# A spectral gate and a GEGLU MLP in one TensorE-bound kernel: operands of the switch on GpSimd's queue, last spectral tiles inside SBUF, a ninth place for half 1's operands

## The chip, the core and the metric

The kernel runs on one core of a Trainium2 chip. The metric is the time of one execution on the device, in microseconds. Matmuls run on TensorE (PE; its weight loads are PEld), element operations on VectorE (DVE) and ScalarE (ACT). SyncE (SP) and GpSimd (POOL) issue the transfers here, each by a queue of its own; in the profile's DMA views SP's transfers are q1, GpSimd's are q0.

## The reference

```python
x = A_x                                        # 1 x 2048 x 576, fp32
g = sigmoid((x * gate_w).sum(-1, keepdims=True))
X = rfft2(x) * (w_r + 1j * w_i)                # 2048 x 289 complex
a = irfft2(X, s=(2048, 576))
h = gelu(x @ w_gate) * (x @ w_up)              # 2048 x 4608, gelu by tanh
b = h @ w_down                                 # 2048 x 576
out = g * a + (1 - g) * b
```

## The kernel before

The matmuls of the MLP and those of the spectral branch run on TensorE in turn, and everything else is laid beside them. Products are made with operands split into a high and a low part (fp32r), three matmuls for one product.

**The MLP.** The 2048 tokens are two halves of 1024; half 0 is done first. After two ordinary blocks of hidden columns come groups; each group makes its gate and up products by seven Strassen-Winograd products (L1334; L1336 for the last 64 rows of the 576) from the token operands `a11`, `a12`, `s2`, `s3`, `s1`, `a22`, `s4` (each a high part `hi`, a low part `lo` and a `tail`) and from weights. Weights are loaded into `low` and `gub` (L1279, L1288), their tails of 96 KB into `gub` or `slot` (L1313), and ScalarE and VectorE split and sum them into one of four slots (L234, L1306, L1321). gelu and the products with it follow (L1360, L1364, L918), then the down products (L933), ScalarE's scaling into one of four `stg` buffers (L965), and `put` (L946): a GpSimd DMA that adds `stg` into `yd` in DRAM.

**The switch.** The operands of half 1 are made early and kept in DRAM, in `kept`. In the last group of half 0, `swap(name)` (L1059, L1060) loads hi (512 KB), lo (512 KB) and tail (256 KB) of each name over half 0's, behind the product that read them last: 21 transfers.

**The spectral branch** is a generator. Each piece of TensorE work ends in a `gap()`, which adds to a credit what the piece took; the generators in `gens` run until the credit is used, then those in `side`. `at(n, fn)` calls `fn` n gaps later, `waits(n)` lets n gaps pass, `step(us)` takes credit. So the order of all engines is set by the credit. Its stages, in order:

- Row FFTs in `rows` (butterflies L93, L98, L101), their tiles sent to `away` in DRAM; the gates.
- `other_operands`: half 1's operands, split by ScalarE's copy (`highs`) and VectorE's subtraction (`rests`, L1138), summed (L1070) and stored to `kept` (L1144, L1151). They lie in a ring of eight places of 256 KB, handed out in turn by `place()`.
- `columns()`: the 16 column blocks kb, in four groups d=0..3 of tiles `G` in `rows`. For each kb a forward product (`product`, L336, six matmuls), a multiplication by the spectral weights `w0`, `w1` (loaded by L326), and a backward product one kb behind. `xh`, `xl` are high and low part of the forward operand (`xl` is L436), `yh`, `yl` those of the backward one (`yl` is L410). GpSimd loads the matrices `col` (L322). `beside()` does, from `side`, the four-point column steps: `forward(d)`, and `backward(d)`, which ends with the tiles of group d going to `home` in DRAM and those of group d+2 coming from `away` (`corner`, L307).
- `inverse_rows(h)`: `fetch(e)` (L634) loads row tiles from `home` into `tmp`, `wtb` and `free_low`, `spin` is their butterfly (L93, L98, L101), `settle` writes them to `rows` (L545), `inverse_stages` does the inverse row FFTs, and `adds` scales eight tiles by the gate into five places (L685 and ScalarE's L683) and adds them to `yd` by GpSimd's queue (L686). For half 0, tiles 2 and 3 of half 1 are fetched and spun at its end.
- At the end `yd` is loaded back (L987) and the last sums are made (L998).

Of the kernel before, what the change touches and what calls it, by code (L numbers as in the profile page):

```python
# [159 lines left out]
def _build(nc, tc, a):  # L160
    with ExitStack() as ctx:
# [126 lines left out]
        def columns():  # L288
# [24 lines left out]

            def store_g(d):
                for e in range(4):
                    q = SW * (d + 4 * e)
                    at(e, lambda q=q, e=e: corner(home[:, q:q + SW], G[d % 2][e], True))

# [30 lines left out]
            def backward(d):  # L349
                while done[0] < 4 * d + 3:  # L350
                    yield None
                yield None
                yield from column_four(G[d % 2], range(4), tmps, 1)
                if d:
                    yield None
                    yield from column_twiddles(G[d % 2], d, LEFT, 1, tmps)
                at(1, lambda: store_g(d))
                if d < 2:
                    yield from waits(6)
                    load_g(d + 2)  # L360
                    yield from waits(7)

# [35 lines left out]
            yield from step()  # L398
            side.append(beside())
            for kb in range(16):  # L400
                was, more = kb > 0, kb + 1 < 16
# [21 lines left out]
                u = product(1, kb - 1, yh, yl) if was else None  # L423
# [3 lines left out]
                if was:  # L427
                    copy(two(tile_of(kb - 1)), u[:, :, :NK])
                    done[0] = kb - 1
                vec.tensor_tensor(vs2[:, 0], zr, zi, ALU.add)  # L430
# [3 lines left out]
                yield from step(0.91)  # L434
                if more:
                    vec.tensor_tensor(xl, tile_of(kb + 1), f(xh), ALU.subtract)  # L436
                yield from step(0.76)
                yield from waits(STEP - 8)
            copy(yh, vs)
# [196 lines left out]
        def inverse_rows(h):  # L636
            sp = zb[0][:, 1664:1664 + SW]

            def spin(e, q):
                yield from butterfly_of(places_of(q)[0], range(4), 1, sp)  # L640

            def settle(e, q):
# [3 lines left out]
            vec.memset(rows.rearrange("p (c k) -> p c k", c=2)[:, :, 8 * KF:], 0.0)  # L646
            if h == 0:
                fetch(0)
                fetch(1)
                yield from waits(3)  # L650
                yield from spin(0, 0)
                yield from along(settle(0, 0), spin(1, 1))
                yield from settle(1, 1)
            yield from inverse_stages()
# [94 lines left out]
        def gap():  # L749
# [7 lines left out]
            if not gens:  # L757
                return
            while credit[0] > 0:
                try:  # L760
# [4 lines left out]
                if v is None:  # L765
                    while side and credit[0] > 0:
# [289 lines left out]
        def swap(name):  # L1056
            hi, lo, tail = ops[name]
            for o, q in ((hi, 0), (lo, 1)):
                nc.sync.dma_start(f(o), kept[name][:, 1024 * q:1024 * (q + 1)].rearrange("p (t k) -> p t k", t=2))  # L1059
            nc.sync.dma_start(f(tail), kept[name][:, 2048:])  # L1060

# [54 lines left out]
        def other_operands():  # L1116

            quads = ops.pop("quads")
            ring = [f(xtl[0]), zb[0][:, 1664:1664 + TB], tmp[:, 3 * TB:4 * TB], *(wtb[:, TB * i:TB * (i + 1)] for i in range(3)),
                    *(free_low[:, TB * i:TB * (i + 1)] for i in range(2))]  # L1120
# [38 lines left out]

            yield from waits(3)  # L1160
            load_xs(1, 2, quads[2])
# [476 lines left out]
```

## Time and profile before

| | |
|---|---|
| runs | 1371.89, 1372.67, 1373.62 us (median 1372.67) |
| profiled execution | 1378.64 us, span 1376.9, mean granted clock 0.987 |
| busy ACT, POOL | 841.7 (61%), 272.2 us (20%) |
| DMA | 263.31 MB in 165553 packets, 191 GB/s |
| q0 (GpSimd) | 47424 packets, 91.51 MB, 42.8% of 16 engines' span |
| q1 (SP) | 117594 packets, 170.05 MB, 38.6% |

The profile is one execution; its times count from the span's start. A granted clock under 1.00 means that TensorE ran slower for a part of a stretch. An idle time is put down to what ended it last; idle time of an engine other than TensorE matters only where TensorE then waits for it. In the chain of waits, "DMA gub<-tails" is the time from a transfer's issue to the work that it released.

### The profile page before, as it was taken

Reading aid. Unit: us, or ns where it says so; the run is one execution under the profiler, and the core shown is the slowest. Engines: PE = TensorE matmul, PEld = TensorE weight load, DVE = VectorE, ACT = ScalarE, POOL = GpSimd, SP = SyncE. Lnnn points to the kernel's source line nnn. Section 1 sums busy time; section 2 is a strip of 40 time slices with the busy share of each in tenths; the row PEclk is TensorE's granted clock in tenths of the full one; section 3 lists DMA queues with packets and bytes.
Section 4 is the critical chain, followed back from the end, with each engine's and each line's share of the span. In section 5 each row is a group of like instructions: output and inputs, shape, how many; then the busy total and the mean of one; then the engine's idle time right before and its main releaser. Section 6 shows DMA issues by size and latency. Waiting matters only on the chain.

```text
span 1376.9 us, 20502 instructions
## 1 busy us (share of the span) xinstructions
PE 1328.2 (96%) x7210; PEld 1164.7 (85%) x7210; DVE 1137.3 (83%) x1750; ACT 841.7 (61%) x1419; POOL 272.2 (20%) x339
## 2 busy tenths in 40 slices
PE   9999999999999988999799999999999999799997
PEld 7888888888888876888678888888788888688896
DVE  7889889879999967596768867876899996699974
ACT  5665655675555657676567767776555557456551
POOL 0011111211111211222221122221111114111132
PEclk9999999999999999999999999999999999899999
DMA  9669998887777899989995797887877779576799
GB/s 348 208 161 218 198 220 190 190 222 137 134 137 136 212 290 253 246 181 289 273 242 137 207 214 162 188 203 152 198 129 136 136 133 240 110 136 132 135 189 230
DMA packets 165553, 263.31 MB, mean 191 GB/s; under 512 B 14346, under 2 KB 79178, under 8 KB 164426
## 3 DMA queue, kind: packets, MB, share of 16 engines
q0 software_dynamic: 47424, 91.51, 42.8%
q1 hardware_dynamic: 117594, 170.05, 38.6%
q8 instruction: 56, 0.92, 0.3%
q10 hardware_dynamic: 432, 0.44, 0.1%
q14 instruction: 47, 0.39, 0.1%
HBM read 141.23 MB, written 123.08 MB: 192 GB/s over the span
## 4 chain that ended last, share of the span: by engine, by line
PE 73%; DMA 16%; DVE 6%; ACT 2%; issue 1%; SPq 0%; DVEq 0%; ACTq 0%
PE pdn L933 25%; PE pgu L1334 18%; PE px L1334 18%; PE pgu L1336 3%; PE px L1336 3%; DMA gub<-tails 3%; DMA tails<-wtb 3%; DMA slot<-tails 2%; DMA tmp<-home 2%; PE pdn L336 1%; DMA wtb<-wt 1%; DMA til<-kept_s 1%; DMA gub<-wf 1%; DMA xlo<-kept_a 1%; DMA tmp<-xs 1%
## 5 line engine op out<-in xcount | busy, mean ns | idle before, releaser
L946 POOL DMA_DIRECT2D yd<-stg x264 | 227.1, 862 | 1040.5 <-ACT stg L965 916.5
L965 ACT ACTIVATE stg<-pdn,omg 128x576 f32<-128x576 f32 x276 | 204.2, 741 | 343.5 <-PE pdn L933 218.9
L933 PEld LDWEIGHTS pdn<-dn,hb 128*128 128x128 f32 x1356 | 194.5, 190 | 10.3 <-ACT stg L965 1.7
L933 PE MATMUL pdn<-dn,hb 128*128 128x288 f32 x1356 | 202.5, 297 | 0.6 <-ACT stg L965 0.6
L1334 PE MATMUL pgu<-xhi,gub 128*128 128x512 f32 x480 | 152.5, 399 | 4.8 <-ACT px L234 2.4
L1334 PE MATMUL pgu<-til,gub 128*128 128x512 f32 x516 | 136.2, 399 | 9.7 <-ACT xraw L234 9.2
L933 PEld LDWEIGHTS pdn<-dn,ext 128*128 128x128 f32 x816 | 124.1, 191 | 14.1 <-DVE low L998 4.2
L933 PE MATMUL pdn<-dn,ext 128*128 128x288 f32 x816 | 132.0, 297 | 3.7 <-DVE low L998 3.7
L933 PE MATMUL pdn<-dn,gub 128*128 128x288 f32 x816 | 130.5, 296 | 0.0
L234 ACT ACTIVATE gub<-low 128x512 fp32r<-128x512 f32 (+1 forms) x163 | 100.9, 621 | 34.0 <-DVE low L1306 28.0
L1334 PEld LDWEIGHTS pgu<-til,gub 128*128 128x128 f32 x516 | 96.1, 191 | 29.9 <-ACT xraw L234 10.1
L933 PEld LDWEIGHTS pdn<-dn,gub 128*128 128x128 f32 x816 | 116.7, 190 | 0.0
L1321 DVE TENSOR_TENSOR gub<-low,gub 128x512 fp32r<-128x512 f32 x151 | 103.3, 684 | 14.7 <-ACT gub L234 14.7
L1334 PE MATMUL px<-xhi,gub 128*128 128x512 f32 x344 | 109.1, 399 | 4.8 <-ACT pgu L234 3.7
L1334 PEld LDWEIGHTS pgu<-xhi,gub 128*128 128x128 f32 x480 | 87.8, 190 | 21.2 <-ACT px L234 3.1
L1334 PE MATMUL px<-til,gub 128*128 128x512 f32 x396 | 102.2, 393 | 0.0
L1334 PE MATMUL pgu<-xlo,gub 128*128 128x512 f32 x240 | 94.8, 395 | 0.0
L1334 PEld LDWEIGHTS px<-til,gub 128*128 128x128 f32 x396 | 72.7, 188 | 14.2
L1334 PEld LDWEIGHTS px<-xhi,gub 128*128 128x128 f32 x344 | 62.8, 190 | 17.0 <-ACT pgu L234 4.5
L1336 PE MATMUL pgu<-til,gub 96*128 96x512 f32 x172 | 69.3, 403 | 6.5 <-DMA gub<-tails 6.5
L933 PE MATMUL pdn<-dn,hx 128*128 128x288 f32 x444 | 70.3, 294 | 0.0
L1306 DVE TENSOR_TENSOR low<-low 128x512 f32<-128x512 f32 x98 | 67.2, 686 | 0.9
(299 smaller groups left out, 2718.0 us busy)
## 6 DMA issues: line engine op xcount, KB each, us to landing
yd<-stg POOLq DMA_DIRECT2D x264, 288.0 KB, 5.6
low<-ws SPq DMA_DIRECT2D x114, 256.0 KB
gub<-wd SPq DMA_DIRECT2D x68, 288.0 KB
gub<-tails SPq DMA_DIRECT2D x179, 96.0 KB
tails<-wtb SPq DMA_DIRECT2D x20, 448.0 KB
slot<-tails SPq DMA_DIRECT2D x59, 96.0 KB
gub<-ws SPq DMA_DIRECT2D x22, 256.0 KB
rows<-away SPq DMA_DIRECT2D x32, 145.0 KB
```

The costliest lines, as they stand in the source:

```text
L234: act.activation(o, i, AF.Copy)
L336: pe.matmul(v[:, al, :NK], cc[d][2 * al + q], two(x)[:, al], start=n == 0, stop=n == 2)
L933: pe.matmul(ps[half], h[:, l, c], d[:, q, half * HD:(half + 1) * HD], start=part == 0 and n == 0, stop=part == 1 and n == 2)
L946: pl.dma_start(yd[u], o, accum_op=ALU.add)
L965: at(n, lambda: put(u, lambda o: act.activation(o.rearrange("p (c k) -> p c k", c=2), v[:, :, 0:HD], AF.Copy, scale=omg[:, u:u + 1]), i == 0))
L1306: vec.tensor_tensor(o, p, q, ALU.subtract)
L1321: vec.tensor_tensor(v[:, 0:5:4], x, f(v[:, 1:4:2]), ALU.subtract)
L1334: pe.matmul(ps, l, x[:, t], start=first and t == 0 and q == 0, stop=False, skip_group_check=True)
L1336: pe.matmul(ps, w[0:96, 512 + P * s:512 + P * (s + 1)], xt[0:96], start=False, stop=True, skip_group_check=True)
```

## The change

1. `swap` issues its 21 transfers from GpSimd (`pl`) instead of SP.
2. The ring for half 1's operands has nine places (tmp 3, tmp 4, the rest as before), and the stage begins one gap later.
3. In `columns()` the backward product of a kb is made earlier, and `xh`, `xl` of the next kb later, in its last two steps: the forward product follows one gap after `xl`. While the loop runs, `side` has first call on the credit (`ops["ahead"]`).
4. `backward` stores its tiles one per gap in the order 1, 2, 3, 0, and loads those of d+2 in the four gaps after. For d=3 the tiles of e=0 and 1 go straight from `rows` to their place in `tmp` and `free_low` (`direct`, eight transfers of 64 partitions x 290), and those of e=2 and 3 to `home`. The other three tiles of e=0 and 1 are loaded from `home` right after the last backward product (`early`); the two fetches at the head of `inverse_rows(0)` are gone.
5. In `inverse_rows(0)` the adds of tiles 4 to 7 run along with `spin(2, 0)` instead of `settle(2, 0)`, and `spin(3, 0)` follows its fetch after seven gaps instead of four. The clearing of a strip of `rows` comes after the first `spin`.

```diff
+            def direct(e):
+                o, x = places_of(e)[0][3].rearrange("p (c k) -> p c k", c=2), two(G[1][e])
+                for c in range(2):
+                    for l in range(2):
+                        nc.sync.dma_start(o[64 * l:64 * l + 64, c], x[64 * c:64 * c + 64, l])
+            def early(e):
+                for x, i, j in places_of(e)[1]:
+                    if i < 3:
+                        nc.sync.dma_start(x[:, 0:3 * SW], home[:, 4 * SW * e:4 * SW * e + 3 * SW])
...
-                at(1, lambda: store_g(d))
+                if d == 3:
+                    return
+                for n, e in enumerate((1, 2, 3, 0)):
+                    at(1 + n, lambda e=e: store(d, e))
+                    if d < 2:
+                        at(5 + n, lambda e=e: load(d + 2, e))
                 if d < 2:
-                    yield from waits(6)
-                    load_g(d + 2)
-                    yield from waits(7)
+                    yield from waits(12)
...
+            ops["ahead"] = True
             for kb in range(16):
...
                 turned(vs, z, 1.0)
+                u = product(1, kb - 1, yh, yl) if was else None
                 yield from step()
-                if more:
-                    while made[0] < (kb + 1) // 4:
-                        yield None
-                    copy(xh, tile_of(kb + 1))
+                if was:
+                    copy(two(tile_of(kb - 1)), u[:, :, :NK])
+                    done[0] = kb - 1
...
                 yield from step(0.91)
                 if more:
+                    while made[0] < (kb + 1) // 4:
+                        yield None
+                    copy(xh, tile_of(kb + 1))
+                yield from step()
+                if more:
                     vec.tensor_tensor(xl, tile_of(kb + 1), f(xh), ALU.subtract)
                 yield from step(0.76)
-                yield from waits(STEP - 8)
+                yield from waits(STEP - 9)
...
             copy(two(tile_of(15)), u[:, :, :NK])
+            set_tmp()
+            for e in range(2):
+                early(e)
             done[0] = 15
             yield None
+            ops["ahead"] = False
             for c in side.pop():
                 yield c
-            yield from waits(2)
-            set_tmp()
+            for e in range(2):
+                at(1 + e, lambda e=e: direct(e))
+                at(3 + e, lambda e=e: store(3, 2 + e))
+            yield from waits(3)
...
             if h == 0:
-                fetch(0)
-                fetch(1)
-                yield from waits(3)
+                yield from waits(1)
                 yield from spin(0, 0)
...
                 yield from adds(0, range(4), places)
-                yield from waits(1)
-                yield from spin(2, 0)
-                yield from along(settle(2, 0), adds(0, range(4, 8), places))
+                yield from along(adds(0, range(4, 8), places), spin(2, 0))
+                yield from settle(2, 0)
                 at(1, lambda: fetch(3, 0))
-                yield from waits(4)
+                yield from waits(7)
                 yield from spin(3, 0)
...
+            ahead = side and ops.get("ahead")
+            while ahead and credit[0] > 0:
+                v = next(side[0], None)
...
             for o, q in ((hi, 0), (lo, 1)):
-                nc.sync.dma_start(f(o), kept[name][...])
-            nc.sync.dma_start(f(tail), kept[name][:, 2048:])
+                pl.dma_start(f(o), kept[name][...])
+            pl.dma_start(f(tail), kept[name][:, 2048:])
...
-            ring = [f(xtl[0]), zb[0][...], tmp[:, 3 * TB:4 * TB], *(wtb ...), *(free_low ...)]
+            ring = [f(xtl[0]), zb[0][...], *(tmp[:, TB * i:TB * (i + 1)] for i in (3, 4)), *(wtb ...), *(free_low ...)]
...
-            yield from waits(3)
+            yield from waits(4)
             load_xs(1, 2, quads[2])
```

The changed kernel's lines lie 14 to 33 further down (L1059 is L1092, L1313 is L1346, L946 is L979, L322 is L336, L686 is L713). Three places in the order of the instructions follow.

SP's queue at the head of the switch, before. `xhi`, `xlo`, `til` are the operands that the swaps fill, `tails` the weights' tails, `ws` the weights:

```order
L1313 DMA gub_72<-tails_109 96x1x256
L1059 DMA xhi_63<-kept_a_99 128x1024
L1059 DMA xlo_65<-kept_a_99 128x1024
L1060 DMA til_302<-kept_a_99 128x512
L1313 DMA gub_72<-tails_109 96x1x256
L1059 DMA xhi_63<-kept_a_100 128x1024
L1059 DMA xlo_65<-kept_a_100 128x1024
L1060 DMA til_302<-kept_a_100 128x512
L1313 DMA gub_73<-tails_109 96x1x256
L1279 DMA low<-ws 128x512
```

GpSimd's queue there, after; `yd<-stg` are the adds of `put`, `col` the column matrices:

```order
L336 DMA xtl_67<-col 128x512
L979 DMA yd_113<-stg_86 128x576
L1092 DMA xhi_63<-kept_a_99 128x1024
L1092 DMA xlo_65<-kept_a_99 128x1024
L1093 DMA til_302<-kept_a_99 128x512
L336 DMA tmp<-col 128x256
L336 DMA gub_73<-col 128x256
L979 DMA yd_114<-stg_87 128x576
L1092 DMA xhi_63<-kept_a_100 128x1024
L1092 DMA xlo_65<-kept_a_100 128x1024
L1093 DMA til_302<-kept_a_100 128x512
L979 DMA yd_115<-stg_84 128x576
```

The three transfers of each name stood ahead of a tail in SP's queue, and stand now ahead of col loads and adds in GpSimd's.

SP's queue between the last columns and the first inverse butterfly, before and then after:

```order
L1279 DMA low<-ws 128x512 x2
L1313 DMA gub_72<-tails_107 96x1x256 x2
L307 DMA home<-rows 64x2x290 x4
L634 DMA tmp<-home 128x2320
L634 DMA wtb<-home 128x1740
L634 DMA low<-home 128x580
L307 DMA home<-rows 64x2x290 x2
L1313 DMA gub_73<-tails_107 96x1x256
L307 DMA home<-rows 64x2x290 x2
L1279 DMA low<-ws 128x512
```

```order
L331 DMA tmp<-home 128x1740
L331 DMA wtb<-home 128x1740
L1346 DMA gub_73<-tails_107 96x1x256
L1346 DMA slot<-tails_107 96x1x256
L1321 DMA gub_794<-wd 128x576 x2
L1312 DMA low<-ws 128x512 x2
L1346 DMA gub_72<-tails_107 96x1x256 x2
L326 DMA tmp<-rows 64x290 x4
L326 DMA low<-rows 64x290 x4
L1346 DMA gub_73<-tails_107 96x1x256
L307 DMA home<-rows 64x2x290 x2
L1312 DMA low<-ws 128x512
```

The loads from `home` moved ahead of a whole set of weights and tails, and small transfers inside SBUF took the place of half the stores and of the last part of the loads.

GpSimd's queue at the adds of half 0, before and then after (`yd<-wtb` and `yd<-low` are the spectral adds, `yd<-stg` the MLP's):

```order
L686 DMA yd_111<-wtb 128x576
L946 DMA yd_123<-stg_84 128x576
L686 DMA yd_112<-wtb 128x576
L686 DMA yd_113<-wtb 128x576
L686 DMA yd_114<-low 128x576
L946 DMA yd_124<-stg_85 128x576
L946 DMA yd_125<-stg_86 128x576
L686 DMA yd_115<-low 128x576
L946 DMA yd_126<-stg_87 128x576
L686 DMA yd_116<-wtb 128x576
L686 DMA yd_117<-wtb 128x576
L946 DMA yd_119<-stg_84 128x576
```

```order
L713 DMA yd_111<-wtb 128x576
L979 DMA yd_123<-stg_84 128x576
L713 DMA yd_112<-wtb 128x576
L713 DMA yd_113<-wtb 128x576
L713 DMA yd_114<-low 128x576
L713 DMA yd_115<-low 128x576
L979 DMA yd_124<-stg_85 128x576
L713 DMA yd_116<-wtb 128x576
L713 DMA yd_117<-wtb 128x576
L713 DMA yd_118<-wtb 128x576
L979 DMA yd_125<-stg_86 128x576
```

After, all eight spectral adds go out with two of the MLP's adds between them; before, six go out with four between them, and two follow. The fetch of the fourth set of tiles (SP's queue) comes behind the eighth now, where it came between the seventh and the eighth.

More of the change, by code (lines that the diff above doesn't have):

```diff
@@ L312, in load_g, with store, load @@
                     at(e, lambda q=q, e=e: corner(away[:, q:q + SW], G[d % 2][e], False))
[L314 to L317, printed above, removed]
+            def store(d, e):
+                q = SW * (d + 4 * e)
+                corner(home[:, q:q + SW], G[d % 2][e], True)
+            def load(d, e):
+                q = SW * (d + 4 * e)
+                corner(away[:, q:q + SW], G[d % 2][e], False)
+            def direct(e):
[7 more added lines that the diff above has]
+                        nc.sync.dma_start(x[:, 0:3 * SW], home[:, 4 * SW * e:4 * SW * e + 3 * SW])
             def load_cc(s, kb):
@@ L640, in spin, with pad @@
                 yield from butterfly_of(places_of(q)[0], range(4), 1, sp)
+            def pad():
+                vec.memset(rows.rearrange("p (c k) -> p c k", c=2)[:, :, 8 * KF:], 0.0)
             def settle(e, q):
@@ L644, in settle @@
                 yield from moved(lambda t, c: (spread(c, t), two(T[t % 4])[:, c, 0:KF]), range(4 * (e % 2), 4 * (e % 2) + 4))
-            vec.memset(rows.rearrange("p (c k) -> p c k", c=2)[:, :, 8 * KF:], 0.0)
             if h == 0:
-                fetch(0)
-                fetch(1)
-                yield from waits(3)
+                yield from waits(1)
                 yield from spin(0, 0)
+                pad()
                 yield from along(settle(0, 0), spin(1, 1))
                 yield from settle(1, 1)
+            else:
+                pad()
             yield from inverse_stages()
@@ L765, in gap @@
                 if v is None:
-                    while side and credit[0] > 0:
+                    while side and not ahead and credit[0] > 0:
                         v = next(side[0], None)
@@ L1118, in other_operands @@
             quads = ops.pop("quads")
-            ring = [f(xtl[0]), zb[0][:, 1664:1664 + TB], tmp[:, 3 * TB:4 * TB], *(wtb[:, TB * i:TB * (i + 1)] for i in range(3)),
+            ring = [f(xtl[0]), zb[0][:, 1664:1664 + TB], *(tmp[:, TB * i:TB * (i + 1)] for i in (3, 4)), *(wtb[:, TB * i:TB * (i + 1)] for i in range(3)),
                     *(free_low[:, TB * i:TB * (i + 1)] for i in range(2))]
```

9 lines of the change are left out of this document (4 added, 5 removed).

## The prediction

> **What bounds the kernel now.** I read the page first (engines, then the forty slices), then a table of windows, then in each window that loses time the waits, the chain of waits and the DMA view. The page says which engine sets the end and where it doesn't run full:
>
> ```profile
> PE 1328.2 (96%) x7210; PEld 1164.7 (85%) x7210; DVE 1137.3 (83%) x1750; ACT 841.7 (61%) x1419; POOL 272.2 (20%) x339
> ...
> PE   9999999999999988999799999999999999799997
> ...
> PEclk9999999999999999999999999999999999899999
> DMA  9669998887777899989995797887877779576799
> ```
>
> TensorE works 96% of the span, so only its gaps can be won, and they lie in a few places (a slice is 34.4 us). The windows put them in microseconds: us, then busy time of PE, PEld, DVE, ACT and POOL, the granted clock, the share of the DMA engines, GB/s.
>
> ```profile
> 475.00:600.00 125.00, 112.31 (x588) 96.62 (x587) 87.41 (x138) 82.25 (x140) 22.73 (x29) 0.96 0.95 256
> 626.00:690.00 64.00, 56.78 (x310) 49.20 (x309) 42.07 (x69) 38.95 (x69) 15.45 (x23) 0.97 1.01 285
> 650.00:725.00 75.00, 64.12 (x330) 54.99 (x329) 49.05 (x78) 44.01 (x75) 15.46 (x21) 0.93 0.96 254
> 725.00:950.00 225.00, 224.97 (x1266) 199.85 (x1265) 178.51 (x281) 162.83 (x272) 48.33 (x65) 1.00 0.79 182
> 950.00:1000.00 50.00, 46.80 (x246) 40.69 (x246) 36.32 (x62) 31.11 (x51) 8.58 (x10) 0.97 0.81 189
> 1175.00:1200.00 25.00, 17.37 (x79) 14.62 (x78) 16.68 (x27) 11.00 (x18) 2.56 (x3) 0.80 0.44 89
> ```
>
> Between 725 and 950 TensorE has no gap at all and the full clock: there the kernel is at its floor. What a window loses I take as its width less busy time times clock, since a matmul at a lower clock is busy for longer: 475–600 loses 125 − 112.31 × 0.96 = 17.2; 650–725 loses 75 − 64.12 × 0.93 = 15.4; 950–1000 loses 4.6; 1175–1200 loses 11.1. These four, 48 us, are the stages that the change touches, and the clock is part of each: behind a gap, matmuls go slowly for a while.
>
> **475–600, the ninth place (A).** Here half 1's operands are made in a ring of eight places. Who waited, for TensorE and VectorE:
>
> ```profile
> PE pgu L1334 <- ACT px L234: 3.3, 2, 2.4
> PE px L1334 <- ACT pgu L234: 2.7, 1, 2.7
> PE pgu L1334 <- DVE gl L1360: 2.3, 1, 2.3
> PE px L1334 <- DVE gl L1360: 2.1, 1, 2.1
> ...
> DVE wtb L1138 <- DMA away<-wtb: 7.8, 1, 7.8
> ...
> DVE low L1138 <- DMA kept_s<-low: 5.4, 2, 4.8
> ```
>
> TensorE waits for VectorE and ScalarE, which were held up in turn by stores that must land before a place is written again. A ninth place means that each place comes back one operand later: it goes for the kept_s wait (5.4), hardly for the wait on the first place (away, 7.8), whose store still lands when it lands. One more gap ahead of the stage, of about 1.6 us of TensorE, takes a little of that one too. I take 5.4/(5.4 + 7.8) = 41% of the 10.4 us of PE waits and of the part of the loss that is clock, about 2 us of it: −5. Ends: 0 (the DMA engines at 0.95 are the limit, and a ninth place only queues another store) and −12 (all four waits and what clock follows them). The operand stores and VectorE's instructions stay as many, so nothing is added.
>
> **626–725, the swaps on GpSimd's queue (B).** Waits of TensorE, then two pieces of the chain of waits, the sync queue's own issue of the first of them, and the DMA view of 626–690:
>
> ```profile
> PE px L1336 <- DMA slot<-tails: 4.9, 2, 2.7
> PE pgu L1336 <- DMA gub<-tails: 3.3, 1, 3.3
> PE pdn L336 <- DVE tmp L436: 1.4, 2, 0.8
> ...
> 670.61 12.94 DMA gub<-tails
> 683.57 9.54 DMA slot<-tails
> ...
> 670.61 0.73 SPq L1313 DMA_DIRECT2D gub<-tails  x1
> ...
> q1 hardware_dynamic: 5346, 13.05, 59.9%
> q0 software_dynamic: 3206, 5.15, 40.8%
> ...
> yd<-stg POOLq DMA_DIRECT2D x11, 288.0 KB, 7.2
> til<-kept_s SPq DMA_DIRECT2D x6, 512.0 KB
> xtl<-col POOLq DMA_DIRECT2D x4, 256.0 KB, 8.5
> ```
>
> The weights' tails are 96 KB and took 12.9 and 9.5 us to land, because they stand in the sync queue (q1) behind 512 KB transfers of the swaps. The 21 swaps carry 7 × 1.28 = 8.96 MB, about half of the 18.25 MB of this window, whose DMA engines are busy throughout. Moved to GpSimd's queue (q0) they are out of the tails' way, since the engines serve both queues in turn; q0 then holds some 14 MB and q1 some 4. What is late next: q0's own work, the adds into yd and the loads of col. Unstalled, TensorE would pass this stretch in about 50 us, and the transfers need 58.7 (the 18.25 MB less 1.5 MB that fell in the stalls, at 285 GB/s), so about 9 us of work stays behind, and now in q0. An add may land late by as much as the four stg buffers cover, four times some 4.8 us between adds (264 over some 1270 us), 19, less the 7.2 it takes: 12 us. A col load is issued 11 to 24 us ahead of its product and takes 8.5. The swapped operands themselves have one whole group, about 38 us of TensorE, before they are read. So 9 us fits, barely. GpSimd issues 21 more, at the page's 862 ns for a DMA of 288 KB (L946) 18 us, beside 15.45 busy in 64: its free time covers that, and without this cover an add would be issued 0.9 us later for each swap ahead of it. The sync engine issues 21 fewer.
>
> ```profile
> L946 POOL DMA_DIRECT2D yd<-stg x264 | 227.1, 862 | 1040.5 <-ACT stg L965 916.5
> ```
>
> Waits for tails are 8.6 of the 15.4 with the slow clock behind them (64.12 × 0.07 = 4.5): 13.1 goes at best. About 3 of it I expect back as single waits for col or stg in q0: −10. Ends: −15 (all) and +5 (q0's surplus of 9 shows on TensorE, and only half of the tails' wait goes).
>
> The row says that a small transfer waits behind big ones of its own queue. The Trainium skill (DMA: Bandwidth & Descriptors, "Issuing engines are not separate DMA queues") speaks against the move: transfers from any engine end on the same 16 DMA engines, and another issuer saves only issue time. By it B would be 0 and the sum 10 us higher. The same page ("Queues, rings and completion order") says that each DMA engine goes round between the queues it has work for, packet by packet, by which the tails do pass; the two busy shares of q0 and q1 in this window fit that, and no row shows a swap in q0.
>
> **Columns, shorter distances (E).** The steps keep their VectorE operations, and the column steps of the groups come ahead of the MLP's side work in each gap; but the low part of the next operand (L436) now comes last, one gap ahead of the forward product, and the backward product earlier.
>
> ```profile
> L436 DVE TENSOR_TENSOR tmp<-rows,tmp x15: 749/754/756, 593.0 to 903.5; 128x580 fp32r<-128x580 f32 x15
> ...
> 626.95 1.58 PE pdn L933 x12
> 628.53 0.81 PE pdn L336 x6
> 629.35 1.39 PE px L1334 x6
> ```
>
> With these prices (12 down matmuls 1.58, 6 of a column product 0.81, 6 of a Strassen product 1.39) I counted in the order of both kernels how much TensorE work lies between L436 and the product that reads it. Before: 1.2 to 4.6 us, and two waits, 1.4 us in all. After: 0 once, 0.23 once, 0.93 twice, else 1.19 to 3.8. VectorE needs 0.75 for the operation and some queue ahead of it; against 1.2 us the shortfalls sum to 1.2 + 0.97 + 2 × 0.27 = 2.7, less little for what is won. I take +2.5; ends 0 (VectorE's queue is empty there) and +6 (15 products with 0.4 each). What covers it is a VectorE busy 178.51 of 225 us.
>
> **950–1000, the last spectral tiles (C).** Waits of VectorE and TensorE, and the chain's piece:
>
> ```profile
> DVE gub L93 <- DMA tmp<-home: 6.0, 1, 6.0
> ...
> PE pgu L1336 <- DMA gub<-tails: 3.2, 1, 3.2
> ...
> 964.42 9.88 DMA gub<-tails
> ```
>
> Before, eight home stores and three loads (1160, 870 and 290 KB) stand in the sync queue ahead of these tails. After, two loads of 870 KB go out 27 us of TensorE sooner, in a stretch where the DMA engines have a fifth free (0.79); half of the last stores are gone, and 8 transfers of 74 KB inside SBUF take the place of 580 KB of loads. What stands ahead of a tail falls from 2.3 MB to about 0.9, and the 3.2 us wait with 1.4 us of clock goes: −4; ends 0 (a tail just behind the early loads is late instead) and −5. No row shows an SBUF-to-SBUF transfer; bounded by a home store's size, twice its cost would be 0.5 MB more, inside the slack.
>
> **1175–1200, the fourth fetch (D).** Waits, then the chain's piece and q0 in 1160–1181:
>
> ```profile
> DVE gub L93 <- DMA tmp<-home: 14.4, 1, 14.4
> ACT xraw L234 <- DVE hb L918: 10.5, 1, 10.5
> ...
> PE pgu L1334 <- ACT xraw L234: 7.6, 1, 7.6
> ...
> 1160.37 20.67 DMA tmp<-home
> ...
> q0 software_dynamic: 1160, 2.37, 63.1%
> ```
>
> The butterfly's wait of 14.4 runs through ScalarE into TensorE with two cushions, 3.9 and 2.9: a wait of 6.8 us would have cost nothing. The fetch is 1160 KB, which at 285 GB/s is 4.2 us; it took 20.67 because accumulating adds filled q0, 63% of all engines. After, the eight adds of the settled tiles are issued within 12 us of TensorE work instead of 26, and the last comes 15 us ahead of the fetch instead of 4 us behind its issue, and between fetch and butterfly lie 8.9 us instead of 6.2. So the wait falls by 2.7 for the distance and by what the adds took, 8 or so: to about 4, under the cushion. −9 of the 11.1; ends −3 (only the distance counts) and −11. What is late next: bunched, adds six to eight rewrite one of five places whose earlier add (about 10 us to land) is under way; that wait of VectorE is within the cushions again unless it passes 6.8 us.
>
> **The end** is the chain from the last adds to their reload, 7.49 us: the last add comes one gap later. +0.5, from −1 to +2.
>
> Sum: −5 − 10 + 2.5 − 4 − 9 + 0.5 = −25. The profiled execution took 1378.64 with a span of 1376.9, 6 above the median of 1372.67; all its terms are gaps of the same places, so I set the sum against the median too: 1372.67 − 25 = 1348 (a span near 1352).
>
> **Rivals.**
> 1. B gains nothing: the 16 engines are the limit and the tails wait as long. For it: DMA share 1.01 in 626–690. Against: GpSimd's adds landed in 7.2 us in the same window in which tails took 9.5 to 12.9. Time 1358. This is also the time by the first of the two rules named under B.
> 2. GpSimd's queue backs up (the slower end). Its place is 626–725: swaps of 512 KB ahead of the adds and col loads, stg runs out, TensorE's down products and column products stop. It decides from the point where an add lands more than 19 us after its issue, or col more than 11. If all of the swaps' 8.96 MB, 31 us at 285 GB/s, lands on the adds and only the 12 us cover is there, it costs 19, the clock behind it (4.5 for 8.6 above) about 10, and the late columns make the early loads and the inverse start late, so that C and half of D are lost: −25 + 10 + 29 + 4 + 4.5 = +22, 1395. Against: swaps come in seven portions with 5 us between them.
> 3. The shorter distances and the bunched adds each make VectorE late, with E at +6 and D at −3: −25 + 3.5 + 6, 1357.
> 4. The ring's stage loses all its waits (A at −12), and B and D two more each: −25 − 7 − 2 − 2, about 1337.
>
> **How the numbers follow.** The sum as made: 0.5 (1340 to 1356). Rival 1: 0.18. Rival 3: 0.12. Rival 4: 0.1. Rival 2: 0.1, of which 0.08 comes out slower by over 0.2% and 0.02 within it; 0.03 of rivals 1 and 3 also ends within it, where A falls short as well. 0.2%, 2.7 us, is about what a measurement of this kernel can tell from no change. Range 1335 to 1364: it leaves out rival 2 and the tails of the others. Faster 0.87, same 0.05, slower 0.08.
>
> **What would show it.** In the profile after: no wait for tails over 1 us in 626–725 and a clock of 0.98 there (B); yd<-stg landing within 12 us, else rival 2; no PE wait for tails at 950–1000 and the first butterfly without a DMA wait (C); the wait on tmp<-home near 1190 below 6 and no PE gap over 3 us there (D); PE's waits for L436's successor 2 to 4 us in all (E); the kept_s waits of VectorE gone in 475–600 (A). The forecast fails most likely at B, where a queue I have not seen with such a load decides 10 us.

## The result, and the profile after

The change makes the kernel faster by 0.67%: the ratio of its runs to those of before is 0.9933 (95% interval 0.9916 to 0.9951), medians 1366.39 and 1376.05 us over 12 runs each. The three runs of before that were shown lay low, at 1372.67. That is 9.2 us where 25 were forecast, and just above the stated range. The profiled execution of the changed kernel took 1365.51 us, its span 1363.4.

The page of the changed kernel, then a table of its windows (columns as before):

```profile
PE 1322.1 (97%) x7210; PEld 1159.4 (85%) x7210; DVE 1137.4 (83%) x1750; ACT 841.8 (62%) x1419; POOL 283.7 (21%) x360
...
PE   9999999999999988999889999999999999999996
...
PEclk9999999999999999999989999999999999999999
DMA  9669998797767899979996698798877779867789
```

```profile
475.00:600.00 125.00, 112.02 (x581) 95.89 (x581) 85.64 (x134) 81.87 (x138) 21.99 (x27) 0.96 0.94 250
626.00:690.00 64.00, 56.31 (x304) 49.31 (x303) 44.26 (x72) 37.88 (x66) 25.82 (x41) 0.93 0.99 294
650.00:725.00 75.00, 65.48 (x350) 56.97 (x350) 52.87 (x84) 45.38 (x78) 22.57 (x34) 0.93 0.97 266
725.00:950.00 225.00, 221.97 (x1248) 196.75 (x1247) 178.93 (x282) 162.15 (x272) 47.74 (x65) 1.00 0.81 189
950.00:1000.00 50.00, 50.00 (x275) 43.96 (x273) 41.24 (x66) 33.65 (x56) 9.67 (x11) 1.00 0.75 150
1150.00:1200.00 50.00, 48.82 (x268) 42.43 (x267) 41.97 (x69) 32.10 (x55) 11.04 (x13) 1.00 0.88 187
```

Slice 35 of the PE row (7 before, the gap at 1176) is full now, while 15 and 16 (475–600) stand at 8 as before, and slices 20 and 21 (650–725), 7 and 9 before, at 8 and 8. The rows say it in numbers: 950–1000 has no gap, 1150–1200 only 1.2 us; 475–600 loses 17.5 (17.2 before), 650–725 14.1 (15.4), and 725–950, which had no gap, loses 3.0.

Kernels whose stages shift against each other are better compared by the same matmuls than by the same microseconds. For the table I took, from each trace, the time between the starts of successive matmuls less their steady pace (230 ns for 512 columns, 131 for 288, 135 for 290), summed between fixed matmuls; the cuts are the matmuls that started at these times before. The last column adds the time behind the last matmul. The names below before and after are those of the experiments, which follow.

| loss, us | to 475 | A: 475–600 | B: 600–725 | E: 725–950 | C: 950–1000 | 1000–1150 | D: 1150–1200 | 1200–1320 | end |
|---|---|---|---|---|---|---|---|---|---|
| before | 8.6 | 20.0 | 17.8 | 1.5 | 5.5 | 0.9 | 11.0 | 0.8 | 11.4 |
| after | 7.6 | 20.7 | 13.8 | 5.2 | 0.3 | 0.9 | 2.2 | 0.8 | 12.5 |
| swap_back | 9.0 | 20.3 | 15.3 | 5.3 | 0.3 | 0.9 | 1.8 | 0.8 | 11.7 |
| swap_act | 7.9 | 20.2 | 22.1 | 4.9 | 0.3 | 0.9 | 1.6 | 0.8 | 12.4 |
| swap_rows | 7.5 | 20.6 | 13.8 | 4.9 | 0.3 | 0.9 | 1.8 | 0.8 | 12.4 |
| swap_split | 7.1 | 21.5 | 27.0 | 7.8 | 0.3 | 0.9 | 1.6 | 0.8 | 12.4 |
| half_swap | 11.4 | 20.5 | 4.5 | 5.5 | 0.3 | 0.9 | 1.8 | 0.8 | 12.1 |
| tails_pool | 6.9 | 21.2 | 11.9 | 7.5 | 0.3 | 0.9 | 1.8 | 0.8 | 11.6 |
| ring8 | 8.9 | 20.9 | 15.0 | 4.9 | 0.3 | 0.9 | 2.1 | 0.8 | 12.2 |
| plain_adds | 8.6 | 12.7 | 12.8 | 4.8 | 0.3 | 0.9 | 2.1 | 1.6 | 12.3 |
| old_fetch | 12.5 | 21.3 | 14.0 | 5.0 | 0.3 | 0.9 | 9.9 | 0.8 | 10.3 |
| old_home | 6.5 | 20.9 | 13.4 | 5.4 | 2.9 | 1.3 | 2.0 | 0.8 | 12.3 |
| no_ahead | 7.6 | 20.7 | 13.7 | 3.6 | 0.4 | 0.9 | 3.8 | 0.8 | 12.9 |
| old_cols | 8.5 | 20.2 | 14.0 | 7.8 | 0.3 | 3.6 | 0.3 | 0.8 | 4.8 |
| cols_side | 8.8 | 19.5 | 15.9 | 1.7 | 0.5 | 0.9 | 3.5 | 0.8 | 13.9 |
| tails_cols | 8.5 | 20.8 | 6.2 | 7.8 | 0.3 | 3.3 | 0.3 | 0.8 | 6.1 |
| tails_side | 9.5 | 19.1 | 13.3 | 1.7 | 0.5 | 0.9 | 5.9 | 0.8 | 14.2 |

Before and after differ by 13.5 us, as their spans do; the profile of before lies 2.6 above its median, that of after 0.9 below, and the first column shows scatter of some us that no change explains.

### The profile page after: what moved, and what is told of

The parts are those of the page before. It is cut to its first block, busy times and chain, and to the rows that moved or that the text cites. A ratio compares the mean times of both kernels' runs of the same rounds, so it can differ in the third digit from the quotient of the medians.

```text
span 1363.4 us, 20503 instructions
## 1 busy us (share of the span) xinstructions
PE 1322.1 (97%) x7210; PEld 1159.4 (85%) x7210; DVE 1137.4 (83%) x1750; ACT 841.8 (62%) x1419; POOL 283.7 (21%) x360
## 4 chain that ended last, share of the span: by engine, by line
PE 69%; DMA 12%; issue 9%; ACT 4%; DVE 3%; POOL 2%; SPq 0%; POOLq 0%; DVEq 0%; ACTq 0%
PE pdn L966 23%; PE pgu L1367 18%; PE px L1367 17%; PE pgu L1369 3%; PE px L1369 3%; POOL yd L979 2%; PE pdn L350 2%; DMA gub<-tails 2%; DMA kept_a<-tmp 2%; DMA slot<-tails 2%; DMA low<-ws 2%; DMA yd<-wtb 1%; DMA rows<-away 1%; ACT stg L998 1%; DMA tails<-wtb 1%
## 5 line engine op out<-in xcount | busy, mean ns | idle before, releaser
L979 POOL DMA_DIRECT2D yd<-stg x264 | 227.4, 864 | 998.3 <-ACT stg L998 871.1
L966 PEld LDWEIGHTS pdn<-dn,hb 128*128 128x128 f32 x1356 | 193.8, 189 | 12.7 <-ACT stg L998 3.9
L1367 PEld LDWEIGHTS pgu<-til,gub 128*128 128x128 f32 x516 | 94.3, 188 | 20.7 <-ACT xraw L234 1.6
L1367 PEld LDWEIGHTS pgu<-xhi,gub 128*128 128x128 f32 x480 | 87.2, 189 | 20.2 <-ACT px L234 4.7
L1367 PEld LDWEIGHTS px<-til,gub 128*128 128x128 f32 x396 | 72.6, 188 | 14.1
```

Of the source, the lines that this page charges most:

```text
L966: pe.matmul(ps[half], h[:, l, c], d[:, q, half * HD:(half + 1) * HD], start=part == 0 and n == 0, stop=part == 1 and n == 2)
L979: pl.dma_start(yd[u], o, accum_op=ALU.add)
L1367: pe.matmul(ps, l, x[:, t], start=first and t == 0 and q == 0, stop=False, skip_group_check=True)
```

## The experiments

Ratios are to the runs of before on the same chip, with 95% intervals.

**The switch (B).** In the changed kernel one tail is waited for longer than any before. PE's wait in 650–725, SyncE's issues, the piece of the chain, and the DMA queues of 668–676 (packets, MB, share of the engines):

```profile
PE px L1369 <- DMA slot<-tails: 6.9, 1, 6.9
...
653.38 5.24 SPq L1321 DMA_DIRECT2D gub<-wd  x1
658.66 3.64 SPq L1312 DMA_DIRECT2D low<-ws  x2
663.41 0.72 SPq L1346 DMA_DIRECT2D slot<-tails  x1
...
670.24 6.78 SPq L340 DMA_DIRECT2D wtb<-wf  x1
...
663.41 22.06 DMA slot<-tails
...
q0 software_dynamic: 934, 2.46, 99.7%
q1 hardware_dynamic: 116, 0.17, 6.1%
```

96 KB took 22 us. Two things are in these rows. Ahead of the tail in SyncE's queue stand loads of weights, 288 KB and twice 256 KB; counted by the lengths of the packets in the trace, 212 of the 256 rows of the two `low<-ws` had not begun when the tail was issued, and the last began at 680.6. And in these 8 us, where the two queues lie furthest apart, GpSimd's got 934 packets through and SyncE's 116, eight to one (in 640–650 it was 1005 to 348), while SyncE itself sat 6.78 us on one issue. So two theories: T, SyncE's queue with the tails in it starves by unequal turns of the queues; V, the engines have more to move than fits, and someone has to wait. P is the prediction.

*swap_back*: `pl.dma_start` in `swap` is `nc.sync.dma_start` again.

> The changed kernel with its 21 swaps issued by SyncE again; all else as changed. Theory T (turns): where both queues have work, a DMA engine serves the eight rows that one GpSimd transfer has on it, and then a single row of the sync queue, so small sync transfers starve behind GpSimd's adds wherever the swaps stand. By it the move was worth only the 3.7 us that the two profiles show for 650-725: 2 to 5 us slower than the changed kernel, 0.995 to 0.997 of the time before. Rival P (the prediction): the tails wait for the swaps in their own queue, and the move gains 10: about 1.000. Rival V (volume): the 16 engines are full, the queue is of no matter: 0.993, as the changed kernel.

0.9934 (0.9916 to 0.9952): no difference from the changed kernel. The waits of 650–725 are three smaller ones again; the last rows are the queues of 668–676:

```profile
PE px L1369 <- DMA slot<-tails: 3.7, 1, 3.7
PE pgu L1369 <- DMA gub<-tails: 2.6, 1, 2.6
...
PE px L1369 <- DMA gub<-tails: 1.1, 1, 1.1
...
q1 hardware_dynamic: 556, 1.49, 55.6%
q0 software_dynamic: 585, 0.87, 52.5%
```

7.4 us against 6.9, and 1.5 us in the table: moving the queue was worth next to nothing. P's time (1.000) is out, and so is T's (0.995 to 0.997); V's (0.993) came. T had said too that the tails starve behind GpSimd's adds wherever the swaps stand; with the swaps on SyncE's queue the packets are 585 to 556.

*swap_act*: the same by `act.dma_start`.

> The changed kernel with its 21 swaps issued by ScalarE, a hardware queue of its own. T: one row at a time like the sync queue, and GpSimd's queue keeps only adds and col; tails land within 10 us, the wait of 6.9 us for them is gone, the loss in 650-725 falls from 13.6 to 8 or less: 0.988 to 0.990. V: the same volume on the same engines: 0.993. If ScalarE's issues hold up its own work (21 of 0.3 to 1.7 us), up to 5 us slower than the changed kernel: 0.996.

0.9970 (0.9957 to 0.9982), slower. TensorE has no wait for tails left between 650 and 725, as T said of a second hardware queue, but ScalarE stood still among its own issues, 8.44 us once and 5.28 another time, until weights and operands had landed, and TensorE behind it (PE's waits, then three rows of ScalarE's timeline):

```profile
PE pdn L966 <- ACT stg L998: 8.7, 2, 7.8
PE pdn L350 <- ACT gub L234: 5.0, 1, 5.0
...
644.73 2.08 ACTq L1092 DMA_DIRECT2D til<-kept_s  x2
...
647.34 0.69 ACT L234 ACTIVATE tmp<-wtb 128x580 fp32r<-128x580 f32 x1 [8.44 <-DMA gub<-wf]
...
662.83 0.63 ACT L1397 ACTIVATE xraw<-xraw 128x512 f32<-128x512 f32 x1 [5.28 <-DMA til<-kept_s]
```

*swap_rows*: `for t in range(2): pl.dma_start(f(o)[:, t], ...512 columns...)`.

> The changed kernel with hi and lo of each swap issued by GpSimd as two transfers of 2048-byte rows instead of one of 4096-byte rows: the same bytes, 14 issues more. T: GpSimd's turn is eight rows whatever their length, so a turn of swaps falls from 1.3 to about 0.8 us and the sync queue's rows pass about 1.6 times as often between them; the tail that took 22 us lands in 14 to 16 and its wait of 6.9 mostly goes: 3 to 6 us faster than the changed kernel, 0.989 to 0.991. V: 0.993. If a turn goes by bytes: 0.993 as well. If GpSimd's issue time counts: 0.995.

0.9929 (0.9908 to 0.9949). It didn't test what it should: the trace has 2240 packets of 4096 bytes in GpSimd's queue between 615 and 710, exactly as without the split, and the tail took 23.57 us. What it does show is that 14 more issues by GpSimd cost nothing.

*swap_split*: two transfers of 64 partitions for each.

> The changed kernel with each swap issued by GpSimd as two transfers of 64 partitions: the same rows and bytes, 21 issues more. If GpSimd's turn is what one transfer has on an engine (T as it stands), a turn falls from eight rows to four, and in the stretch where the swaps fill the queue the sync queue passes about 1 row to 4 instead of 1 to 8; the tail lands in 12 to 16 us instead of 22 and 3 to 6 us are won (0.989 to 0.991). If a turn is eight rows of the queue, whatever transfer they belong to: 1 to 8 as before and 0.993. V: 0.993.

1.0023 (1.0004 to 1.0042), the only kernel here that is slower than before. The DMA engines were as full as ever in 626–690 (1.04) but moved 241 GB/s where the changed kernel moves 294, a tail took 26.7 us, and col was late too. The rows are its window and its PE waits in 650–725:

```profile
626.00:690.00 64.00, 55.98 (x294) 48.08 (x292) 40.90 (x66) 34.82 (x59) 31.55 (x55) 0.95 1.04 241
...
PE px L1373 <- DMA slot<-tails: 10.8, 2, 9.9
PE pdn L350 <- DMA xtl<-col: 3.9, 1, 3.9
```

Neither reading of a turn forecast this; why 64 partitions carry less was not tried further.

*half_swap*: the loop in `swap` only over `(hi, 0)`; the lo parts of half 1 are left out.

> The changed kernel without the loads of the lo parts in the swaps (seven transfers, 3.67 MB; half 1 is then computed with the wrong low parts, the work stays the same). V: 3.67 MB at 285 GB/s is 13 us of all engines, and the loss of 650-725, 13.6, falls to 3 or less: 10 us faster than the changed kernel, 0.986. T alone: fewer turns of swaps, but the adds' turns stay, and a tail still takes over 12 us: 3 to 5 us faster, 0.990.

0.9878 (0.9851 to 0.9906). Its window of 650–725, and its queues in 668–676:

```profile
650.00:725.00 75.00, 72.12 (x401) 63.22 (x400) 61.32 (x97) 52.26 (x90) 21.51 (x31) 1.00 0.98 249
...
q0 software_dynamic: 862, 1.79, 97.3%
q1 hardware_dynamic: 122, 0.21, 7.8%
```

In these 8 us the queues are as unequal as in the changed kernel (7 to 1), and yet no wait for a tail is left in 650–725; the loss of B falls from 13.8 to 4.5. So 3.67 MB less take most of the loss, as V said. The time alone does not decide, its interval holds T's 0.990 as well as V's 0.986; and the missing bytes were GpSimd's, so they lightened its queue too.

*tails_pool*: `prep`'s tails by `pl` from the first swap to twelve gaps behind the last.

> The changed kernel with the ten weight tails that fall within the switch (from the first swap to twelve gaps behind the last) issued by GpSimd too, in its queue's own order among swaps and adds. No byte more or less. Theory T (turns: eight rows of GpSimd's queue to one of the sync queue): the tails leave the starved queue, land in about 10 us like everything in GpSimd's queue, and the 6.9 us wait for slot<-tails is gone; the loss of 650-725 falls from 13.6 to 7 or less: 5 to 8 us faster than the changed kernel, 0.988 to 0.9905. Theory V (volume: the engines have more to move than fits into the switch): the wait comes back at col, the adds or the weights, and the time is that of the changed kernel, 0.993.

0.9915 (0.9892 to 0.9937): between the two, and not separated from the changed kernel by itself. Its window and waits:

```profile
650.00:725.00 75.00, 66.96 (x362) 57.75 (x361) 54.91 (x87) 46.59 (x80) 28.91 (x42) 0.98 1.02 274
...
PE px L1372 <- DMA slot<-tails: 3.2, 1, 3.2
...
PE px L1372 <- DMA gub<-tails: 1.6, 1, 1.6
```

The waits for tails are 4.8 us instead of 6.9, and the engines move more here (274 GB/s against 266). By this window the loss is 9.4 instead of 14.1, but by the same matmuls only 11.9 instead of 13.8, and the columns behind it lose 2.3 more. By itself this does not show that the queue matters; tails_cols, below, does.

**Half 1's operands (A).** *ring8*: `tmp[:, 3 * TB:4 * TB]` alone in the ring; the later start is kept.

> The changed kernel with eight places (tmp 3 alone, without tmp 4) in the ring for half 1's operands. Theory S: that stage waits for stores to land in 6 to 10 us from full DMA engines, and a ninth place only moves the wait to the next store: within 2 us of the changed kernel, 0.992 to 0.9945. Rival P (the prediction): the ninth place is worth 5 us: 0.997.

0.9940 (0.9921 to 0.9960), A at 20.9 against 20.7: the ninth place does nothing that can be measured. In the changed kernel VectorE's waits of 475–600 have only changed their names:

```profile
DVE wtb L1171 <- DMA kept_s<-wtb: 6.8, 1, 6.8
...
DVE wtb L1171 <- DMA away<-wtb: 4.2, 1, 4.2
DVE low L257 <- DMA kept_s<-low: 4.0, 1, 4.0
```

*plain_adds*: `accum_op` left out in `put` while `other_operands` runs, so that these adds are plain stores.

> The changed kernel with the MLP's adds into yd written plainly, without accumulation, while half 1's operands are made (the sums of these tokens are then wrong; the work of the engines stays). Theory S (that stage waits for stores to land because the DMA engines are full): half of the adds' engine time there, about 12 us of all engines, goes, VectorE's waits for kept_s and kept_a stores shrink below 3 us each, and the loss of 475-600 falls from 20 to 12 or less: 7 to 10 us faster than the changed kernel, 0.986 to 0.988. Rival: the stage is bound by the order of VectorE's and ScalarE's work, not by landings: within 2 us, 0.993.

0.9869 (0.9842 to 0.9896). The loss of A falls from 20.7 to 12.7, and its DMA share from 0.94 to 0.88; VectorE's longest wait for a kept_s store halves:

```profile
475.00:600.00 125.00, 117.27 (x624) 101.71 (x623) 91.52 (x144) 88.22 (x150) 20.40 (x31) 0.97 0.88 262
...
DVE wtb L1173 <- DMA kept_s<-wtb: 3.3, 1, 3.3
```

So 8 of the 20.7 us that this stage loses go when the adds give the DMA engines less to do, and none that can be measured goes by a place more in the ring. What makes the other 12.7 was not taken apart.

**The inverse (C and D).** *old_fetch*: `spin(2, 0)`, then `along(settle(2, 0), adds(...))`, `waits(4)`.

> The changed kernel with the old end of half 0's inverse: adds of tiles 4 to 7 beside settle, the fourth fetch four gaps before its butterfly. As predicted (D): adds and fetch collide again, the butterfly waits 10 us or more, and the loss of 1150-1200 goes from 2 to 8 to 11: 6 to 9 us slower than the changed kernel, 0.998 to 1.000. Rival: without the late stores of the last columns the same order does no harm: 0.993.

0.9987 (0.9969 to 1.0004): 7 us of the gain are gone. VectorE's wait and the chain's piece are those of before, to half a us (14.4 and 20.67):

```profile
DVE gub L93 <- DMA tmp<-home: 14.9, 1, 14.9
...
1160.07 21.11 DMA tmp<-home
```

In the changed kernel the same wait is 4.5 us, under the cushion of 6.8:

```profile
DVE gub L93 <- DMA tmp<-home: 4.5, 1, 4.5
```

The place of the adds and the longer distance were taken back together; which of them is worth what stays open.

*old_home*: four stores and the two fetches again instead of `early` and `direct`.

> The changed kernel with the old way of the last tiles: all four of d=3 stored to home, then the two fetches at the head of the inverse (no early loads, nothing inside SBUF). As predicted (C): the tails wait behind these transfers, the loss of 950-1000 goes from 0.3 to 4 to 6: 4 to 5 us slower than the changed kernel, 0.9965. Rival: only the order of stores and loads mattered, not the volume in the sync queue: 0.993.

0.9963 (0.9947 to 0.9980): about 4 us slower by the medians, and a wait for a tail is back in 950–1000:

```profile
PE px L1368 <- DMA slot<-tails: 2.3, 1, 2.3
```

Its profile is its fastest execution (1366.89, median 1370.87) and shows only 2.6 of the 4 us in C (2.9 against 0.3); where the rest lies is not seen.

**The columns (E) and the end.** *old_cols*: the loop's body as before the change, with the side steps' first call. *no_ahead*: the changed kernel without `ops["ahead"] = True`. *cols_side*: both of these.

> The changed kernel with the old order inside a column step (backward product late, high and low part of the next operand early); the side steps keep their first call. As predicted (E): the new order costs 2.5 to 4 us between 725 and 950 by operands that come too late; with the old one this loss falls from 5 to about 1: 3 to 4 us faster than the changed kernel, 0.990 to 0.9905. Rival: the loss there (ScalarE's stg waits, 2.5 us) comes from the side steps' first call, and nothing changes: 0.993; or the backward groups now finish later and move the end: slower by 2 or more.

> The changed kernel without the side steps' first call on the credit (they come behind the main generator, as before the change); the new order inside a column step stays. Theory F: the first call bunches the side's VectorE and ScalarE work into single gaps and so makes the 5 us loss between 725 and 950 (ScalarE's stg waits, the late operand); without it this loss falls to 2 or less: 3 us faster than the changed kernel, 0.991. Theory O: the order inside the step makes it, by the shorter distance from the low part to its product: the loss stays at 4 to 6, 0.993. If the column steps then come late and the branch ends later: slower, 0.995 or more.

> old_cols without the first call: both parts of the column loop as before the change, the stores, early loads and transfers inside SBUF as changed. F: the loss of 725 to 950 falls from the 7.8 of old_cols to 2 or less, and the branch still ends early: 5 us faster than old_cols, 0.9865. O: as old_cols, 0.990. If the first call is what made the branch end early, the 7 us at the end come back: 0.993.

old_cols 0.9902 (0.9886 to 0.9917), no_ahead 0.9930 (0.9907 to 0.9953), cols_side 0.9941 (0.9923 to 0.9958). old_cols gave the expected time by luck, for another reason: its columns lose more (7.8), so does 1000–1150 (3.6), and the end loses 7.7 less. The last adds that are loaded back at the end went out in the changed kernel, and then in old_cols, at

```profile
1339.07 1.74 POOL L713 DMA_DIRECT2D yd<-tmp  x2 [0.22 <-issue]
```

```profile
1331.59 2.25 POOL L712 DMA_DIRECT2D yd<-tmp  x2
```

and with them 7.5 us earlier TensorE waits nowhere in the last down products, where in the changed kernel it waited 4.6 for their reload:

```profile
PE pdn L966 <- DVE low L1031: 4.6, 3, 2.7
```

The four kernels make a square. Without the first call the new order costs 1.9 us in the columns (3.6 against 1.7); with it the columns lose 5.2 (new order) and 7.8 (old). And only old order with first call brings the branch in early enough to free the end (4.8, the others 12 to 14). F is half right: the first call does cost 1.6 to 6 us in the columns. That it pays at the end was in none of the theories.

*tails_cols*: tails_pool and old_cols together; *tails_side*: that without the first call.

> tails_pool and old_cols together: the switch's tails by GpSimd and the old column order. If both gains are real and add: 6 us faster than the changed kernel, 0.9885. If the switch is bound by volume alone and the columns' loss is not their order: 0.992 to 0.993.

> tails_cols without the first call. F: 5 us faster than tails_cols, 0.9825. O: as tails_cols, 0.986. If the branch then ends late: 0.990.

tails_cols 0.9861 (0.9845 to 0.9877), median 1355.94 us: the fastest of all kernels here, faster than the changed one and than before. That is 9.9 us faster than the changed kernel by the ratios, where the sum of the two gains was put at 6. Against old_cols, from which only the queue of the ten tails differs and no byte, the loss of B falls from 14.0 to 6.2; the tails in the chain of waits take 10.5 and 8.1 us where they took 22.6 and 20.0. So V alone, by which the queue is of no matter, is out as well. The rows are 600–725 of old_cols, then of tails_cols:

```profile
600.00:725.00 125.00, 116.04 (x632) 102.24 (x631) 90.98 (x146) 80.85 (x139) 41.22 (x62) 0.96 0.96 254
...
600.00:725.00 125.00, 120.31 (x674) 106.18 (x673) 97.37 (x156) 87.58 (x150) 50.10 (x74) 1.00 0.98 264
```

tails_side 0.9919 (0.9898 to 0.9941): the branch ends late again, as its expectation's last case said, and in 600–725 TensorE waits for col, as it does in cols_side too (8.3 us), and little for tails:

```profile
PE pdn L350 <- DMA xtl<-col: 6.2, 1, 6.2
```

B loses 13.3 there. So what the tails' queue is worth (2 us in tails_pool, 8 between old_cols and tails_cols, 3 between cols_side and tails_side) differs with the order of the columns; it may hang on which of their loads fall into the switch, but that was not tried.

## Why the prediction was right or wrong

- **B, −10 forecast, −4 by the two profiles, nothing that the runs can tell (swap_back).** The failing step is "Moved to GpSimd's queue (q0) they are out of the tails' way, since the engines serve both queues in turn". What is in the slower tail's way besides the swaps is SyncE's own: before the change, too, four loads of weights, 1.1 MB, were issued right ahead of the tail of 683.57,

```profile
679.88 1.05 SPq L1288 DMA_DIRECT2D gub<-wd  x2
681.27 1.03 SPq L1279 DMA_DIRECT2D low<-ws  x2
```

and they stayed there. With the swaps in GpSimd's queue, SyncE's got 116 packets through in 8 us against 934, so these loads and the tail behind them starved instead of being freed: the wait was 6.9 us, the tail took 22. The sum "about 9 us of work stays behind, and now in q0" does not follow from its own row: TensorE's work in 626–690 is 56.78 × 0.97 = 55 us and not 50, which leaves 4. What the runs show in its place is two things at once. Bytes: with 3.67 MB less the stage loses 4.5 instead of 13.8 (half_swap). And the tails' own queue: with the old columns and the ten tails on GpSimd's queue it loses 6.2 instead of 14.0, no byte less (tails_cols against old_cols). With the new columns the same move of the tails won only 1.9 (tails_pool, 11.9); why is open.

  Rival 1 gave the right gain for this term, none, but its reason, the limit of the engines, is only part of it. The rule that I set against the move (the Trainium skill, DMA: Bandwidth & Descriptors, "Issuing engines are not separate DMA queues") gave 0, and swap_back agrees. The same page of the Trainium skill ("Queues, rings and completion order") says that an engine drains a whole packet of many descriptors before it changes queues. I had read that as fair turns; 934 to 116 would fit turns of unequal length, but swap_back has 585 to 556, and no run here shows how long a turn is.
- **A, −5 forecast, +0.7 and nothing measurable (ring8).** The failing step is "it goes for the kept_s wait (5.4)". It gave the wait to another store (kept_s<-wtb 6.8, kept_s<-low 4.0). The end that I had put at 0, "the DMA engines at 0.95 are the limit", was nearer, and plain_adds shows 8 us of it.
- **D, −9: −8.8.** The wait fell to 4.5, where about 4 was worked out; old_fetch, which undoes distance and adds together, takes 7 us back.
- **C, −4: −5.2**, and old_home takes 4 back by the medians. No wait for tails is left in 950–1000, as forecast.
- **E, +2.5: +3.7.** The size came near by luck. The cost was to be TensorE's waits for the operand's low part (L436, now L455), 2 to 4 us in all. In 560–960 that wait is shorter than the 1.4 us of before:

```profile
PE pdn L350 <- DVE tmp L455: 0.9, 1, 0.9
```

The new order does cost 1.9 us without the first call (no_ahead against cols_side), but such waits are only 0.5 of it (L454 in no_ahead, in 725–950). The first call, which the text mentions without a price, costs 1.6 more. How the two cost this stays open; of the changed kernel's 3.0 us of gaps in 725–950, 1.3 are a wait for a tail, 0.9 the one above and 0.8 one for `stg`.
- **End, +0.5: +1.1.** The size was near, and too small to be told from scatter. That the end could be freed by a branch a few us earlier I did not see.
- **Rival 2** (GpSimd's queue backs up) did not happen, though one of its two signs just did. The last column is the median from issue to landing in 626–690:

```profile
yd<-stg POOLq DMA_DIRECT2D x11, 288.0 KB, 10.7
...
xtl<-col POOLq DMA_DIRECT2D x3, 256.0 KB, 11.6
```

The adds stay far under the 19 us that it named, col passes its 11 by a little; TensorE waited for no col there, and ScalarE's `stg` for no add.
- **The base**: the sum was set against 1372.67; the median of 12 runs is 1376.05, so 3.4 us of the distance between forecast and result are the base.
- **Small slips**: the swaps are 9.18 MB, not 8.96. In C, "from 2.3 MB" counts the three loads alone; with the six stores ahead of that tail it is 3.3. Before the change seven spectral adds, not six, went out with four of the MLP's between them, and one followed.

So of −25, the terms for the late stages came out within 1.5 us each with their mechanism, that for the columns without it, and −15 rested on two stages with DMA shares of 0.95 and 1.01, where I priced waits and not transfers.

## What to carry to other kernels

In the two stages here whose DMA share was 0.95 and 1.01, a wait in the profile named the transfer that came last and not the cause: one more place in the ring, or another queue for the large transfers, gave the wait another name and won nothing. Two things did shorten them: less work for the DMA engines (half_swap, plain_adds), and another queue for the small transfer that TensorE waits for (tails_cols). So before you move what seems to stand in a transfer's way, list all that was issued ahead of it in its queue, and ask what will still stand there. And follow a side branch to its end: in old_cols a few us earlier there were worth more than what its steps cost on the way.

## What the runs showed that was not expected

- Two loaded queues did not share the engines evenly where GpSimd's held the swaps: 934 packets to 116 in the 8 us of the widest gap (862 to 122 in half_swap). With the swaps on SyncE's queue it was 585 to 556 in the same 8 us.
- Swaps in transfers of 64 partitions instead of 128: 241 GB/s at full engines in 626–690, where 294 were moved in the changed kernel.
- The swaps' 2048-byte rows (the tails of the operands, and in swap_rows all) went through GpSimd's queue in packets of 4096 bytes.
- With the swaps on ScalarE's queue, ScalarE did no work of its own for up to 8.44 us around their issues; which of its waits were the issues' is not shown.
